# Attention with mixed heads: the scores and the product with v in four TensorE visits per row group

## The chip, the cores and the metric

The kernel runs on one core of one Trainium2 chip. The metric is the device time in microseconds (us) of one execution; the median of three executions stands for the kernel. Engines: TensorE (PE; PEld is its weight load), VectorE (DVE), ScalarE (ACT), GpSimd (POOL), SyncE (SP, which here only issues DMAs).

## The reference, cut to what matters

```python
scores = scale * q @ k.T                            # 4 batches, 12 heads, 448 x 448, head size 64
scores = einsum('bhij,hg->bgij', scores, w_pre)     # first mixing, over the heads
attn = softmax(scores)                              # max, exp, sum, divide
attn = einsum('bgij,gf->bfij', attn, w_post)        # second mixing, over the heads
x = attn @ v                                        # "a times v", then 1792 tokens x 768
x = ((x @ w1) * (x @ w2)) @ w3 @ w_out
out = square(relu(x @ w_in)) @ w_out2
```

Everything is float32 at the borders. Products are made in three terms of high and low halves.

## The kernel before, in words

**Row groups and blocks.** Each batch has four row groups of 110, 110, 110 and 118 query rows (`SUP`, 16 in all, called s). A row group is cut into blocks of ten rows (the last one may have eight; `BLK`, 180 in all, called u). A block holds 10 rows x 12 heads = 120 partitions, so that both mixings over the heads are matmuls with a 120 x 120 matrix. `first[s]` is the first block of row group s. A row group lasts 11 or 12 blocks.

**What happens to a row group.** `qk(s, p)` (line 228) makes the scores of a pair of heads p (six pairs) into one PSUM tile of two banks of which there is one (`ps_s`); its six matmuls work on the two halves of 64 rows of the array. `evict_s` (line 246) copies them on ScalarE into the row group's tile S. `regroup(u)` (line 274) brings ten rows of all heads by a DMA on SyncE's queue into the tile Bt (five buffers). Then per block: `premix` (line 281, the first mixing, TensorE, into one of three PSUM tiles p), `negmax` (VectorE), `expo` (ScalarE), `norm` (VectorE), `split_h` (GpSimd; on ScalarE for some blocks while k is split) and `split_l` (VectorE for even blocks, GpSimd for odd ones) make the halves EH and EL, `postmix` (line 371, the second mixing, TensorE, into one of two PSUM tiles o), `at_h` (ScalarE) and `at_l` (VectorE) raise the result into the halves ATh and ATl. When all blocks of a row group are there, `av(s, p, part)` (line 477) multiplies by v: 24 matmuls for a pair of heads, each on 64 columns of the array, three pairs of heads into the one PSUM tile a. `put_xh` (ScalarE) and `put_xl` (VectorE) take x out of it as two halves, `store_x` (SyncE) writes them to memory.

**The order.** It is written by hand. A loop over slots u (line 1320) issues in each slot: loads; `at_h` of block u - 5; in odd slots the first mixing of blocks u + 1 and u + 2; `negmax(u)`; events of the kind FIRST; `expo(u)`; the norms and splits of blocks u - 2 and u - 3; the second mixing of block u - 4; `at_l` of block u - 5; events of the kinds MID and LOW; events of the kind END; last `regroup(u + 5)`. Every engine works through its instructions in this order. The events (from line 546) say in which slot the pieces of `qk`, `evict_s`, `av` and so on stand. Before, the six pieces of `qk` of row group s are spread evenly over a row group's slots (`qs`, line 557), one to a slot, the copy `evict_s` one slot later; the pieces of `av` of an earlier row group stand in the same slots behind them (`at_qk`, line 597). A visit below is a slot in which TensorE leaves the mixings for `qk` or `av`.

**Other pieces that the change touches.** `load_q`, `split_q` and `split_ql` run nine, five and four slots ahead of the score pieces that need them. The k of the next batch is loaded and split in slots `ks` (line 571). `scale_v` (line 439) finds the scale of v by two small matmuls, for which it borrows the bank of the a tile. `split_v` and `split_vl` split v for row group 4b.

Of the kernel before, what the change touches and what calls it, by code (L numbers as in the profile page):

```python
# [18 lines left out]
P = 128  # L19
CP = 112  # L20
F64_BIAS = 2.0 ** -112
NR = 10
ROWS = (110, 110, 110, 118)
LEAD = 5
LAG = 4
EG = 7
EW = 66
TB = 4
# [6 lines left out]
def talking_heads_attention_moe_moe2(  # L35
# [55 lines left out]
    def psum(pool, tag, dt=F32):  # L91
        return pool.tile([P, 512], dt, tag=tag, name=tag)
# [346 lines left out]
    def scale_v(b, i):  # L439

        m = vsum[b]
        if i == 0:
            nc.vector.tensor_reduce(m[:CP, 6:7], m[:CP, 0:6], axis=AX.X, op=ALU.max)
        elif i == 1:
            t = pav[4 * b - 1, 1] if b else psum(ps_a, "a")
            vps[b] = pt = t[:, 512 - P :]
            nc.tensor.transpose(pt[:1, :CP], m[:CP, 6:7], ident[:CP, :CP])
        elif i == 2:
            nc.vector.tensor_reduce(m[:1, 7:8], vps[b][:1, :CP], axis=AX.X, op=ALU.max)
        elif i == 3:  # L450
            nc.tensor.matmul(vps[b][:, :1], ones[:1], m[:1, 7:8], start=True, stop=True)
        else:
            up, lo = pow2(vps.pop(b)[:, :1], 14, "vs")
            nc.vector.tensor_scalar(
                xs[:, b : b + 1], lo, wunscale, 2.0 ** XSH, op0=ALU.mult, op1=ALU.mult
            )
            Vsc[b] = up
# [87 lines left out]

    events = {}
    LOAD, FIRST, MID, LOW, END = range(5)

    def at(slot, kind, f, *a):
        events.setdefault(slot, []).append((kind, len(events), f, a))  # L550

    low_k, crowded, copies = set(), set(), []
    for s in range(2, NSUP):
        b = SUP[s][0]
        base = first[s - 1]
        L = first[s] - base
        qs = [base - 4 + p * L // NDC for p in range(NDC)]
        made = list(qs)
        if s == 2:
            made[:3] = base - 5, base - 2, base - 1  # L560
        for p in range(NDC):
            at(made[p], END, qk, s, p)
            copies.append((base - 2 if s == 2 and p == 0 else made[p] + 1, s, p))
            if p % 3 == 0:
                at(qs[p] - 9, LOAD, load_q, s, p // 3)
                at(qs[p] - 5, MID, split_q, s, p // 3, None)
                if p == 0 and qs[p] - 4 in low_k:
                    crowded.add(qs[p] - 3)
                at(qs[p] - 4 + (qs[p] - 3 in crowded), LOW, split_ql, s, p // 3)
        if s % 4 == 0:  # L570
            ks = [(first[s - 2] + 4) // 2 * 2 + 2 * p for p in range(NDC)]
            full.update(range(ks[0], ks[-1] + 4))
            for p in range(NDC):
                assert ks[p] + 1 < qs[p]
                at(ks[p], MID, split_k, b, p, None)
                at(ks[p] + 1, LOW, split_kl, b, p)
                low_k.add(ks[p] + 1)
                at(ks[p] - 4, LOAD, load_k, b, p)
    for slot, s, p in copies:
        at(slot, MID if slot in crowded else FIRST, evict_s, s, p)  # L580
    for b in range(B):
# [3 lines left out]
        for hg in range(2):  # L585
            for i in range(3):
# [3 lines left out]
                if b == B - 1:  # L590
                    at(f + 3 * hg + i + 13, MID, split_v, b, hg, i)
                    at(f + 3 * hg + i + 14, LOW, split_vl, b, hg, i)
    qk_at = sorted(x for x in events if any(e[2] is qk for e in events[x]))
    for s in range(NSUP - 1):
        for p in range(NDC):
            lo = first[s + 1] + LAG + 1
            at_qk = [x for x in qk_at if lo <= x < lo + SUP[s + 1][3]]
            slot = at_qk[p] if len(at_qk) == NDC else lo + (0, 1, 3, 5, 6, 7)[p]
            if s % 4 == 0 and s < NSUP - 4:
                b = SUP[s][0]  # L600
                assert slot - 2 > first[s] + 13
                at(slot - 2, MID, split_v, b, *divmod(p, 3))
                at(slot - 1, LOW, split_vl, b, *divmod(p, 3))
            for part in range(2):
                at(slot, END, av, s, p, part)
            if p % 3 == 2:
                at(slot + 1, FIRST, put_xh, s, p // 3)
                at(slot + 1, MID, put_xl, s, p // 3)
                if s < NSUP - 2:
                    at(slot + 2, END, store_x, s, p // 3)  # L610

    for b in range(B):
        for i, slot in ((1, 10), (3, 12)):
            at(first[4 * b] + slot, END, scale_v, b, i)

    last = NSUP - 1
    for p in range(NDC):
        for part in range(2):
            at(first[last] + TB + LAG + 1 + (2 * p + part) * (NB - first[last] - TB) // 12,
               END, av, last, p, part, (0, TB * NR))  # L620


    order = ExitStack()
# [693 lines left out]

    mlp_start = first[NSUP - 1] - 4
    early = iter(())
    for u in range(NB + LAG + 2):  # L1320
        if u == NB - LEAD:
            limit[0] = len(chunks)
            load_to(2 + LOADS)
        if u == mlp_start:
            kst.close()
            pools["w"] = ctx.enter_context(tc.tile_pool(name="wp", bufs=2, side="right"))
        if u in W_LOADS:
            load_to(W_LOADS.index(u) + 1)
        if u == c0:
            early = (x for x in pair_steps(0, None) if x[2])  # L1330
        if u - mlp_start in X_HIGH:
            load_x(0, X_HIGH.index(u - mlp_start))
        if u == NB - LEAD + 1:
            for b in range(B):
                load_x(1, b)
        work = sorted(events.pop(u, []), key=lambda e: e[0])

        def do(now):
            for kind, _, f, a in work:
                if kind == now:  # L1340
                    f(*a)

        do(LOAD)
        if 0 <= u - LAG - 1 < NB - LAG:
            at_h(u - LAG - 1)
        if u in AHEAD:
            postmix(u - LAG)
        if u % 2:
            for x in (u + 1, u + 2):
                if x < NB:  # L1350
                    premix(x)
        if u in FILL:
            keep_busy(FILL[u])
        if u < NB:
            negmax(u)
        do(FIRST)
        if u < NB:
            expo(u)
        if u % 2 == 0 and 0 <= u - 2 < NB:
            norm(u - 2)  # L1360
        if 0 <= u - 2 < NB:
            split_h(u - 2)
            if low_on_pool(u - 2):
                split_l(u - 2)
        if 0 <= u - 3 < NB and not low_on_pool(u - 3):
            split_l(u - 3)
        if 0 <= u - LAG < NB and u not in AHEAD:
            postmix(u - LAG)
        if 0 <= u - LAG - 1 < NB - LAG:
            at_l(u - LAG - 1)  # L1370
        do(MID)
        do(LOW)
        for eng, cost, f in islice(early, STEPS.get(u, 0)):
            f()
        do(END)
        if NB <= u < NB + LAG:
            assert next(early, None) is None
            allow[0] = place["w1", 2]
            at_h(u - LAG)
            at_l(u - LAG)  # L1380
            first_tile(u - NB)
        if u + LEAD < NB:
            regroup(u + LEAD)
# [923 lines left out]
```

## Time and profile before

| | |
|---|---|
| median of three runs | 1222.35 us (1222.11 to 1223.85) |
| profiled execution | 1222.48 us, span 1220.8 us |
| TensorE busy | 1206.9 us, 99% of the span |
| VectorE, ScalarE, GpSimd busy | 948.8, 804.5, 587.6 us |
| TensorE's clock | granted in full in all 40 slices of the span |
| attention | about the first 430 us; the MLPs behind it |

The span reaches from the first to the last instruction, the time of an execution a little further. A line such as L380 is a line of the kernel: L284 is the first mixing, L380 the second, L241 the scores, L494 a times v, L248 the score copy, L396 and L402 the raising into ATh and ATl. In a timeline a record is an instruction, or several alike (x2); the records of one engine overlap, because matmuls are pipelined, so starts are compared with starts. In the chain of waits each piece is the time by which the work that ended last was carried by that line.

### The profile page before, as it was taken

The numbers are of one execution on the slowest core, as the hardware profiler recorded it, in microseconds if no ns is written. First come the engines' busy times: TensorE is split into PE (matmuls) and PEld (weight loads), VectorE is DVE, ScalarE is ACT, GpSimd is POOL, SyncE is SP. The second block draws the span as 40 slices with busy tenths as digits, with TensorE's granted clock in tenths as the row PEclk, the third lists the DMA queues.
The fourth block names the chain that finished last, engine by engine and source line by source line (L and its number), as shares of the span: only waits on it lengthen the run. The fifth ranks groups of instructions, "written<-read, shape, count | busy, mean of one in ns | idle before, by whom it ended". The sixth has DMA issues, their size and how long they took to land.

```text
span 1220.8 us, 26222 instructions
## 1 busy us (share of the span) xinstructions
PE 1206.9 (99%) x9904; PEld 746.7 (61%) x9904; DVE 948.8 (78%) x1690; ACT 804.5 (66%) x1620; POOL 587.6 (48%) x569
## 2 busy tenths in 40 slices
PE   8999999999999999999999999999999999999998
PEld 3666676676676665555557985555555555666665
DVE  6988899888889956766675876697778775999773
ACT  6887888878888735654464545567878876654430
POOL 3898788889879510110001311446233424666340
PEclk9999999999999999999999999999999999999999
DMA  6466555655645843755543537344478659656562
GB/s 193 129 161 163 138 146 132 171 126 155 172 119 162 242 128 95 175 127 156 134 134 112 189 120 242 127 159 166 160 251 290 240 185 314 207 162 187 171 196 79
DMA packets 139843, 205.02 MB, mean 168 GB/s; under 512 B 33764, under 2 KB 114788, under 8 KB 139716
## 3 DMA queue, kind: packets, MB, share of 16 engines
q1 hardware_dynamic: 136020, 200.01, 55.4%
q10 hardware_dynamic: 3136, 2.40, 0.8%
q8 instruction: 78, 1.28, 0.4%
q0 software_dynamic: 560, 0.93, 0.4%
q14 instruction: 49, 0.40, 0.1%
HBM read 114.60 MB, written 50.16 MB: 135 GB/s over the span
## 4 chain that ended last, share of the span: by engine, by line
PE 90%; DMA 4%; DVE 3%; ACT 1%; issue 0%; SPq 0%; ACTq 0%; POOL 0%
PE mm L1248 25%; PE mm L2113 16%; PE mm L1861 16%; PE p L284 9%; PE o L380 7%; PE mm L1525 5%; PE s L241 5%; PE a L494 4%; DMA Bt<-S 2%; PE p L1248 2%; DVE ATl L402 1%; DMA x<-x_d 1%; DVE EL L367 1%; DVE st L298 1%; ACT E L306 0%; DMA vraw<-in_v_dram 0%
## 5 line engine op out<-in xcount | busy, mean ns | idle before, releaser
L1248 PE MATMUL mm<-x,w 128*128 128x448 f16 x1044 | 197.7, 352 | 0.0
L1248 PEld LDWEIGHTS <-w 128*128 128x128 f16 x1152 | 112.2, 98 | 105.2 <-issue 1.0
L1861 PE MATMUL mm<-x,wq 128*128 128x448 f16 x882 | 169.2, 352 | 0.0
L284 PE MATMUL p<-Bt,wpre_k 120*120 120x448 f32 x360 | 159.4, 560 | 5.7 <-DMA Bt<-S 3.1
L2113 PEld LDWEIGHTS <-ao 128*128 128x128 f16 x1176 | 115.0, 98 | 76.0
L380 PEld LDWEIGHTS <-EH 120*112 120x112 f16 (+1 forms) x1440 | 124.3, 130 | 44.6 <-issue 37.2
L353 POOL TENSOR_SCALAR EH<-E,st 120x448 f16<-120x448 f32 (+1 forms) x152 | 113.0, 751 | 47.7 <-DVE st L336 35.6
L1861 PEld LDWEIGHTS <-wq 128*128 128x128 f16 x882 | 86.0, 98 | 79.6
L402 DVE TENSOR_TENSOR ATl<-o,ATh 112x480 f16<-112x480 f32 x180 | 116.1, 645 | 23.9 <-ACT ATh L396 22.9
L396 ACT CAST ATh<-o 112x480 f16<-112x480 f32 x180 | 101.2, 562 | 45.7 <-PE o L380 40.7
L306 ACT ACTIVATE E<-p,st 120x448 f32<-120x448 f32 x180 | 116.1, 645 | 21.5 <-DVE st L298 13.1
L380 PE MATMUL o<-wph,EH 120*112 120x120 f16 x720 | 124.1, 219 | 1.2 <-DVE ATl L402 1.1
L380 PE MATMUL o<-wph,EL 120*112 120x120 f16 x720 | 122.0, 216 | 0.0
L380 PE MATMUL o<-wpl,EH 120*112 120x120 f16 x720 | 122.0, 216 | 0.0
L365 POOL TENSOR_TENSOR EL<-F,EH 120x448 f16<-120x448 f32 (+1 forms) x90 | 104.6, 1162 | 33.7 <-issue 20.4
L298 DVE TENSOR_REDUCE st<-p 120x1 f32<-120x448 f32 x180 | 110.2, 612 | 2.6 <-PE p L284 2.4
L1248 PE MATMUL mm<-h,M 128*128 128x448 f16 x576 | 110.2, 353 | 0.0
L2113 PE MATMUL mm<-x,ao 128*128 128x384 f16 x588 | 96.5, 326 | 0.0
L2113 PE MATMUL mm<-ow,ao 128*128 128x384 f16 x588 | 96.0, 326 | 0.0
L380 PEld LDWEIGHTS <-EL 120*112 120x112 f16 x720 | 93.6, 130 | 0.0
L367 DVE SCALAR_TENSOR_TENSOR EL<-E,st,EH 120x448 f16<-120x448 f32 (+1 forms) x90 | 82.9, 921 | 10.3 <-POOL EH L353 9.9
L1248 PEld LDWEIGHTS <-M 128*128 128x128 f16 x576 | 55.9, 98 | 52.0 <-DVE M L1435 0.8
(264 smaller groups left out, 2535.1 us busy)
## 6 DMA issues: line engine op xcount, KB each, us to landing
Bt<-S SPq DMA_DIRECT2D x176, 210.0 KB
raw<-in_moe_w_out_dram SPq DMA_DIRECT2D x24, 768.0 KB
g<-ev SPq DMA_DIRECT2D x64, 224.0 KB
gt<-g SPq DMA_DIRECT2D x56, 256.0 KB
raw<-in_moe_w_in_dram SPq DMA_DIRECT2D x16, 768.0 KB
raw<-in_moe_w_dram SPq DMA_DIRECT2D x14, 768.0 KB
raw<-in_moe_w_dram SPq DMA_DIRECT2D x16, 512.0 KB
kept_out<-xa SPq DMA_DIRECT2D x16, 384.0 KB
```

Of the source, the lines that this page charges most:

```text
L284: nc.tensor.matmul(pt[: n * H, :S], wpre_k.rearrange("p t g -> p (t g)")[: n * H, : n * H], Bt.pop(u)[: n * H], start=True, stop=True,)
L298: nc.vector.tensor_reduce(nsum[u][:n, 0, j : j + 1], Pp[u][:n, :S], axis=AX.X, op=ALU.max, negate=True)
L306: nc.scalar.activation(e[:n], Pp.pop(u)[:n, :S].rearrange("p (a b) -> p a b", a=EG), AF.Exp, bias=t[:n, 0, j : j + 1], scale=1.0, accum_ou ...
L353: nc.gpsimd.tensor_scalar(seven(EH[u][:n]), Ex[u][:n], inverse(u), 1.0, op0=ALU.mult, op1=ALU.mult)
L365: nc.gpsimd.tensor_tensor(a, f, b, op=ALU.subtract)
L367: nc.vector.scalar_tensor_tensor(a, e, inverse(u), b, op0=ALU.mult, op1=ALU.subtract)
L380: nc.tensor.matmul(pt[:CP, c * n : (c + 1) * n], a[:n, c * CP : (c + 1) * CP], w[:n, :n], start=(i == 0), stop=(i == 2),)
L396: nc.scalar.copy(ATs[s][0][:, :, :, m * NR : m * NR + nr], src)
L402: nc.vector.tensor_tensor(ATs[s][1][:, :, :, a], src, ATs[s][0][:, :, :, a], op=ALU.subtract)
L1248: nc.tensor.matmul(pt[:, :S], w[a][:, cs], x[z][:, sl], start=(c == 0 and i == 0), stop=(c == len(parts) - 1 and i == 2),)
L1861: nc.tensor.matmul(pt[:, :S], w[:, a, c * P : (c + 1) * P], xop(t, b, kb, c), start=(start and c == 0 and m == 0), stop=(c == 2 and m == 2 ...
L2113: nc.tensor.matmul(pt[:, :OH], y[:, a, q * P : (q + 1) * P], ow[g, q][kb][:, w], start=(start and q == 0 and m == 0), stop=(q == NQ - 1 an ...
```

## The change

From row group 3 on, the six score pieces stand in four visits: a, a + 3, a + 6 and at most a + 9, where a is the first odd slot from `first[s - 1]` - 4 on. In slots a and a + 6 there is a double visit: a score piece, its copy `evict_s` at once in the same slot, all three pairs of heads of `av` for one half (hg) of row group s - 3, then a second score piece, whose copy follows in the next slot behind `expo`. In a + 3 and in the last one stands a single score piece. `early_high` calls `at_h` of block u - 4 in the slot of the double visit, ahead of the copy, and not at the start of the next slot. For row groups 13 and 14, which have no scores beside them, `av` stands in two visits and not in six. In a slot behind a slot with a visit, `postmix` comes ahead of `premix`. The splits of v come in neighbouring slots, `ks` starts two slots earlier, `scale_v` takes a PSUM tile of its own ring, and kinds END to END + 3 order scores, a times v, second scores, and stores with `scale_v`.

```diff
--- before.py
+++ after.py
@@ -442,8 +442,7 @@
         if i == 0:
             nc.vector.tensor_reduce(m[:CP, 6:7], m[:CP, 0:6], axis=AX.X, op=ALU.max)
         elif i == 1:
-            t = pav[4 * b - 1, 1] if b else psum(ps_a, "a")
-            vps[b] = pt = t[:, 512 - P :]
+            vps[b] = pt = psum(ps_a, "a")[:, 512 - P :]
             nc.tensor.transpose(pt[:1, :CP], m[:CP, 6:7], ident[:CP, :CP])
         elif i == 2:
             nc.vector.tensor_reduce(m[:1, 7:8], vps[b][:1, :CP], axis=AX.X, op=ALU.max)
@@ -545,22 +544,41 @@
 
     events = {}
     LOAD, FIRST, MID, LOW, END = range(5)
+    raised = set()
+
+    def early_high(u):
+        if BLK[u][1]:
+            at_h(u)
+            raised.add(u)
 
     def at(slot, kind, f, *a):
         events.setdefault(slot, []).append((kind, len(events), f, a))
 
     low_k, crowded, copies = set(), set(), []
+    double, from_pool = {}, {}
     for s in range(2, NSUP):
         b = SUP[s][0]
         base = first[s - 1]
         L = first[s] - base
-        qs = [base - 4 + p * L // NDC for p in range(NDC)]
-        made = list(qs)
         if s == 2:
-            made[:3] = base - 5, base - 2, base - 1
+            qs = [base - 4 + p * L // NDC for p in range(NDC)]
+            made = [base - 5, base - 2, base - 1] + qs[3:]
+        else:
+            a = (base - 4) | 1
+            qs = made = [a, a, a + 3, a + 6, a + 6, min(a + 9, base + L - 6)]
+            double[s] = (a, a + 6)
         for p in range(NDC):
-            at(made[p], END, qk, s, p)
-            copies.append((base - 2 if s == 2 and p == 0 else made[p] + 1, s, p))
+            if made.count(made[p]) == 1:
+                at(made[p], END, qk, s, p)
+                copies.append((base - 2 if s == 2 and p == 0 else made[p] + 1, s, p))
+            elif p % 3 == 0:
+                at(made[p], END, early_high, made[p] - LAG)
+                at(made[p], END, qk, s, p)
+                at(made[p], END, evict_s, s, p)
+            else:
+                at(made[p], END + 2, qk, s, p)
+                copies.append((made[p] + 1, s, p))
+                crowded.add(made[p] + 1)
             if p % 3 == 0:
                 at(qs[p] - 9, LOAD, load_q, s, p // 3)
                 at(qs[p] - 5, MID, split_q, s, p // 3, None)
@@ -568,7 +586,7 @@
                     crowded.add(qs[p] - 3)
                 at(qs[p] - 4 + (qs[p] - 3 in crowded), LOW, split_ql, s, p // 3)
         if s % 4 == 0:
-            ks = [(first[s - 2] + 4) // 2 * 2 + 2 * p for p in range(NDC)]
+            ks = [(first[s - 2] + 2) // 2 * 2 + 2 * p for p in range(NDC)]
             full.update(range(ks[0], ks[-1] + 4))
             for p in range(NDC):
                 assert ks[p] + 1 < qs[p]
@@ -590,34 +608,32 @@
                 if b == B - 1:
                     at(f + 3 * hg + i + 13, MID, split_v, b, hg, i)
                     at(f + 3 * hg + i + 14, LOW, split_vl, b, hg, i)
-    qk_at = sorted(x for x in events if any(e[2] is qk for e in events[x]))
     for s in range(NSUP - 1):
+        b, lo = SUP[s][0], first[s + 1] + LAG + 1
         for p in range(NDC):
-            lo = first[s + 1] + LAG + 1
-            at_qk = [x for x in qk_at if lo <= x < lo + SUP[s + 1][3]]
-            slot = at_qk[p] if len(at_qk) == NDC else lo + (0, 1, 3, 5, 6, 7)[p]
+            hg, i = divmod(p, 3)
+            slot = double[s + 3][hg] if s + 3 in double else lo + (3, 7)[hg]
             if s % 4 == 0 and s < NSUP - 4:
-                b = SUP[s][0]
-                assert slot - 2 > first[s] + 13
-                at(slot - 2, MID, split_v, b, *divmod(p, 3))
-                at(slot - 1, LOW, split_vl, b, *divmod(p, 3))
+                assert slot - 4 > first[s] + 13
+                at(slot - 4 + i, MID, split_v, b, hg, i)
+                at(slot - 3 + i, LOW, split_vl, b, hg, i)
             for part in range(2):
-                at(slot, END, av, s, p, part)
-            if p % 3 == 2:
-                at(slot + 1, FIRST, put_xh, s, p // 3)
-                at(slot + 1, MID, put_xl, s, p // 3)
+                at(slot, END + 1, av, s, p, part)
+            if i == 2:
+                at(slot + 1, FIRST, put_xh, s, hg)
+                at(slot + 1, MID, put_xl, s, hg)
                 if s < NSUP - 2:
-                    at(slot + 2, END, store_x, s, p // 3)
+                    at(slot + 2, END + 3, store_x, s, hg)
 
     for b in range(B):
         for i, slot in ((1, 10), (3, 12)):
-            at(first[4 * b] + slot, END, scale_v, b, i)
+            at(first[4 * b] + slot, END + 3, scale_v, b, i)
 
     last = NSUP - 1
     for p in range(NDC):
         for part in range(2):
             at(first[last] + TB + LAG + 1 + (2 * p + part) * (NB - first[last] - TB) // 12,
-               END, av, last, p, part, (0, TB * NR))
+               END + 1, av, last, p, part, (0, TB * NR))
 
 
     order = ExitStack()
@@ -1317,6 +1333,7 @@
 
     mlp_start = first[NSUP - 1] - 4
     early = iter(())
+    turned = {x for x in events if any(y[2] in (qk, av) for y in events[x])}
     for u in range(NB + LAG + 2):
         if u == NB - LEAD:
             limit[0] = len(chunks)
@@ -1341,9 +1358,9 @@
                     f(*a)
 
         do(LOAD)
-        if 0 <= u - LAG - 1 < NB - LAG:
+        if 0 <= u - LAG - 1 < NB - LAG and u - LAG - 1 not in raised:
             at_h(u - LAG - 1)
-        if u in AHEAD:
+        if u in AHEAD or u - 1 in turned and 0 <= u - LAG < NB:
             postmix(u - LAG)
         if u % 2:
             for x in (u + 1, u + 2):
@@ -1364,7 +1381,7 @@
                 split_l(u - 2)
         if 0 <= u - 3 < NB and not low_on_pool(u - 3):
             split_l(u - 3)
-        if 0 <= u - LAG < NB and u not in AHEAD:
+        if 0 <= u - LAG < NB and u not in AHEAD and u - 1 not in turned:
             postmix(u - LAG)
         if 0 <= u - LAG - 1 < NB - LAG:
             at_l(u - LAG - 1)
@@ -1372,7 +1389,8 @@
         do(LOW)
         for eng, cost, f in islice(early, STEPS.get(u, 0)):
             f()
-        do(END)
+        for kind in range(END, END + 4):
+            do(kind)
         if NB <= u < NB + LAG:
             assert next(early, None) is None
             allow[0] = place["w1", 2]
```

## Rows read from the trace of the kernel before

**Rows 1.** Chain of waits, 300 to 345 us: shares by line, one piece (start, us, what)
```profile
by line: PE p L284 37.0%; PE o L380 28.4%; PE s L241 17.7%; PE a L494 16.9%; issue 0.1%
...
301.25 1.59 PE p L284 x4
```

**Rows 2.** Stretches: us, busy PE, PEld, DVE, ACT, POOL (xcount), clock, DMA share, GB/s
```profile
160.00:210.00 50.00, 49.53 (x665) 35.17 (x663) 46.79 (x96) 41.44 (x91) 45.05 (x48) 1.00 0.58 150
210.00:260.00 50.00, 50.00 (x647) 35.10 (x645) 41.19 (x94) 40.35 (x94) 39.64 (x47) 1.00 0.58 151
```

**Rows 3.** TensorE's timeline around one visit: start, us, what
```profile
303.26 0.22 PE L380 MATMUL o<-wph,EL 120*112 120x120 f16 x1
303.40 0.45 PE L241 MATMUL s<-kh,qh 64*110 64x448 f32 x2
303.69 0.37 PE L241 MATMUL s<-kl,qh 64*110 64x448 f32 x2
303.90 0.37 PE L241 MATMUL s<-kh,ql 64*110 64x448 f32 x2
304.20 0.24 PE L494 MATMUL a<-ATh,Vh 112*64 112x110 f16 x2
304.27 0.22 PE L494 MATMUL a<-ATl,Vh 112*64 112x110 f16 x2
...
304.75 0.22 PE L494 MATMUL a<-ATh,Vl 112*64 112x110 f16 x2
304.90 0.26 PE L380 MATMUL o<-wph,EH 120*112 120x120 f16 x1
305.00 0.22 PE L380 MATMUL o<-wpl,EH 120*112 120x120 f16 x1
```

**Rows 4.** Chain of waits, 400 to 470 us: start, us, what
```profile
400.30 0.63 PE o L380 x12
400.93 0.70 PE a L494 x24
401.63 0.77 PE o L380 x12
...
404.07 7.56 DMA Bt<-S
...
421.40 8.20 DMA x<-x_d
```

**Rows 5.** TensorE's timeline, scores followed by the first mixing
```profile
47.81 0.37 PE L241 MATMUL s<-kh,ql 64*110 64x448 f32 x2
48.11 1.76 PE L284 MATMUL p<-Bt,wpre_k 120*120 120x448 f32 x4
```

**Rows 6.** Groups by line, 150 to 400 us: ScalarE's score copy (busy us, mean ns, idle before)
```profile
L248 ACT COPY S<-s 110x896 f32<-110x896 f32 (+1 forms) x56 | 51.2, 914 | 4.7 <-PE s L241 4.3 <-DMA vraw<-in_v_dram 0.2
```

**Rows 7.** VectorE's timeline: the low half of xt
```profile
218.56 0.50 DVE L522 SCALAR_TENSOR_TENSOR xt<-a,xt 128x330 f16<-128x330 f32 x1 [0.82 <-DMA Bt<-S]
```

**Rows 8.** SyncE's timeline: DMA issues
```profile
220.48 0.82 SPq L278 DMA_DIRECT2D Bt<-S  x1
...
295.61 1.47 SPq L203 DMA_DIRECT2D qraw<-in_q_dram  x1
297.18 0.82 SPq L278 DMA_DIRECT2D Bt<-S  x1
```

**Rows 9.** All of TensorE's waits, 60 to 400 us: total us, times, longest
```profile
PE o L380 <- DVE ATl L402: 0.8, 2, 0.5
PE p L284 <- ACT E L306: 0.2, 1, 0.2
PE p L284 <- ACT ATh L396: 0.2, 1, 0.2
```

**Rows 10.** GpSimd's timeline: two low halves of k
```profile
300.67 1.12 POOL L196 TENSOR_TENSOR kl<-kraw,kh 128x448 fp32r<-128x448 f32 x1
...
305.01 2.09 POOL L196 TENSOR_TENSOR kl<-kraw,kh 128x448 fp32r<-128x448 f32 x1
```

## The prediction

> **What bounds the kernel now.** I read the page's engine table first: TensorE is the busiest engine by far. Busy is not the same as bound, so next the chain of waits over 300 to 345 us, a stretch of the attention: its line of shares holds four TensorE lines and 0.1% of anything else [rows 1]. Third, the table by stretches says who would be next: between 160 and 260 us TensorE has half a microsecond of idle time in a hundred, VectorE is at 46.79 and 41.19 of 50 us, and GpSimd at 45.05 and 39.64 [rows 2]. So a microsecond taken from TensorE in the attention is a microsecond of time, as long as VectorE, GpSimd and the deliveries of the tile Bt can follow; the first two have 6% to 21% in hand.
>
> Fourth, TensorE's own timeline, start to start, shows what could be taken. Inside a kind of matmul the starts are regular [rows 3]: 0.05 us in the second mixing (0.63 for twelve [rows 4]), 0.21 in the scores (303.69 to 303.90), 0.048 in a times v (ten pairs of records from 304.27 to 304.75). At each border between kinds something is lost:
> - second mixing into scores: 0.14 instead of 0.05, and the first scores pair holds 0.29 instead of 0.21: 0.17;
> - scores into a times v: 0.30 instead of 0.21, and 0.07 instead of 0.05: 0.11;
> - a times v into second mixing: 0.15 instead of 0.05, and 0.10 instead of 0.05: 0.15. The chain gives 0.77 for such a mixing against 0.63 [rows 4], so I use 0.14;
> - second mixing into a times v alone: 0.70 for 12 pairs that need 0.58 [rows 3, 4]: 0.12;
> - scores into the first mixing: 0.30 instead of 0.21 [rows 5]; what the first mixing itself then loses doesn't show in that row. I take 0.14 in all, as on leaving a times v; at 0.09, the least, the sum below would be 2.7 us better (53 more such borders after than before).
>
> **The change, part by part.** *Borders.* Written out from the slot tables of both versions, the old order enters scores 84 times, goes on from there to a times v 79 times, enters a times v alone 16 times, leaves a times v 95 times and leaves scores for something else 5 times: 84 x 0.17 + 79 x 0.11 + 16 x 0.12 + 95 x 0.14 + 5 x 0.14 = 38.9 us. The new order has 26 double visits (13 row groups, two each: scores, three heads' a times v, scores), 32 visits with scores alone and 11 with a times v alone: 58 x 0.17 + 26 x 0.11 + 26 x new + 58 x 0.14 + 11 x 0.12 + 11 x 0.14 = 23.7 + 26 x new. The new border, a times v into scores, is in no row. Its nearest rows are 0.11 (scores into a times v) and 0.31 (leaving for the mixing and entering from it, 0.14 + 0.17); I take 0.17, the entry into scores, since what follows the border is the same instruction. That makes 28.1 us, **10.8 us saved**, between 7.1 and 12.3. (The Trainium skill, TensorEngine Tiling (Array Packing), section Key Properties, says that a change of tiling mode drains the engine, and a change of tile within a mode does not. By it the new border is one drain; it gives no duration, and with one drain priced as entry into scores the sum stays 10.8.)
>
> *Where that doesn't count.* From 404 us on, the chain runs through deliveries, Bt from 404.07 and x until 429.60 [rows 4]. Four of the six visits for row group 14 disappear inside that stretch, 4 x 0.26 = **1.0 us** that I take off.
>
> *The second scores piece of a double visit* needs the one score buffer, so ScalarE must copy the first piece out while TensorE does a times v. If it is late, TensorE stops, and behind it the next second mixing. The first piece ends about 0.9 us after the mixing before it, the copy takes 0.91 [rows 6], a times v runs for 1.75 us (36 pairs). ScalarE has 0.56 us of raising (at_h, now called ahead of the copy) to do in the first 0.9. It is left with 0.8 us: nothing is paid, unless ScalarE comes 0.8 us late. After the visit its work bunches: the xt copy can't start before a times v ends, then the exponential, the second copy and the next raise stand in line. VectorE's subtraction for ATl comes as much later, and the mixing two slots on needs that output buffer. Counted through with these durations it holds with a tenth or two to spare; I cost it at nothing beside the next item, which falls in the same place.
>
> *Bt and SyncE's queue.* The work between visits is now uneven. From the end of the mixing before a double visit: visit 0.89 + 1.75 + 0.17 + 0.63 + 0.14 = 3.58, mixing 0.63; a pair of slots with first mixings 1.59, two mixings and a single visit (0.17 + 0.63 + 0.14), 3.79; a pair without a visit, 1.59 + 1.26 = 2.85; the next two first mixings start at 10.85 and about 11.65. Their Bt tiles are issued behind the store of xt, which waits for VectorE's xt. That is ready at 2.64 + 0.22 (last a times v) + 0.5 (ScalarE, taken as VectorE's for the same columns) + 0.50 [rows 7] = 3.86, and the next Bt went out 1.42 us after it (219.06 to 220.48 [rows 8]): at 5.3. Its own issue takes 0.82, and in two of three cases a load of q follows, 1.47 [rows 8]: the second Bt goes out at 7.6, with 4.05 us to land. How long a landing takes is in no row; the tile issued at 297.18 [rows 8] was used by the second first mixing of the pair at 301.25 [rows 1], at about 302.05, without a wait, so 4.87 bounds it. Missing are thus between 0 and 0.8 us in each half row group. Nothing else shortens the far end, and none of TensorE's waits between 60 and 400 us is one for Bt [rows 9], so most landings beat that bound; I take 0.15. 26 x 0.15 = **3.9 us** off.
>
> *VectorE and GpSimd.* 10.8 us over 13 row groups is 0.83 for one of about 25 us. The stretch of each batch in which k and v are split (some 60 us, as 150 to 210) would be asked to run 2.0 us shorter with VectorE at 94% already [rows 2]; the three v splits now stand in neighbouring slots, and the k splits start two slots earlier. Between nothing and all of it is lost; I take a quarter, 0.5 us for each of three batches, **1.5 us**.
>
> *At nothing:* the second mixing put ahead of the first behind a visit is an order on TensorE alone; it delays the first mixing by 0.63, which the three p buffers cover while VectorE still has a maximum to take, and otherwise it would be part of the 0.15. The k loads two slots earlier on SyncE's queue wait for the same splits, which are two slots earlier too. The bank that scale_v now takes for itself waits for the xt of the slot before, one slot of over 2 us earlier.
>
> **Sum:** 10.8 - 1.0 - 3.9 - 1.5 = 4.4 us. The profiled execution took 1222.48 us (span 1220.8), 0.13 above the median of the three runs: 1218.1 against the first, **1218.0 us** as a median. A measurement of this kernel can tell about 0.2%, 2.4 us, from no change.
>
> **The rivals.** *It all comes through:* landings stay under 4 us and VectorE follows: 10.8 - 1.0 = 9.8, 1212.5 (1211.0 with the new border at 0.11). For it: no wait on Bt between 60 and 400 us today. Against it: the 4.05 us are less than the only bound. Chance 0.20.
>
> *No change, because VectorE and GpSimd become the bound:* all 2.0 us of the three split stretches are lost, 10.8 - 1.0 - 3.9 - 6.0 = -0.1, 1222.5. A GpSimd subtraction took 1.12 us once and 2.09 another time [rows 10], so work there grows when it is squeezed against VectorE's. (The Trainium skill, SBUF — State Buffer, section SBUF: two separate sides, says that a VectorE operation with two SBUF inputs and a GpSimd operation hold the shared ports exclusively, the other waiting for the whole instruction. By that rule their two busy times cannot be packed closer, which is this rival.) The same time comes out where *the change doesn't do what it says*: if the new border costs 0.31, the sum is 7.1 - 1.0 - 5.4 = 0.7, 1221.7. Together 0.20.
>
> *Slower:* each double visit holds SyncE's queue (the store waits for xt, the q load and Bt stand behind it), and the Bt for the next double visit lands late by 0.7 us, as the 4.87 allow. 26 x 0.7 = 18.2: 1222.4 - 9.8 + 18.2 = 1230.8. It decides from (10.8 - 1.0) / 26 = 0.38 us a half group on. For it: Bt landings of 7.56 us appear when the queues are full [rows 4]. Against it: up to 400 us the first mixing is not held now. Chance 0.20.
>
> **How the numbers follow.** The forecast (1215.2 to 1219.9) has 0.40. Faster by over 0.2% is 0.40 + 0.20 = 0.60, within it 0.20, slower 0.20. The likeliest case's own range is 1215 to 1220; the range for 8 in 10 runs from 1212.0, a little inside the best end, to 1226.0, which takes in the unchanged case and the near part of the slower one; outside stay some 0.05 below and 0.13 above.
>
> **What would show it.** Right: in TensorE's timeline two scores pieces round 72 records of a times v, the border between at 0.17 more than the regular step, and the row-group period shorter by 0.3 to 0.8 us. TensorE's waits show Bt for the first mixing behind a pair without a visit, a few us in total. Wrong: the border at 0.25 or more; waits of scores on the score copy (ScalarE late by over 0.8 us); second mixing held by ATl or EL for more than a microsecond a row group, which would put the bound on VectorE or GpSimd; or Bt waits of 10 us and more, which would make it slower. If the gain shows at 400 us but not at the end, the delivery stretch took it.

## The result: 1.4% slower

The changed kernel takes 1239.12 us (1237.43 to 1243.01), the kernel before, beside it, 1222.97: a ratio of 1.0137, 95% interval 1.0108 to 1.0165, 16 us more where 4.4 less was forecast. The profiled execution took 1240.67 us, its span is 1239.0. The lines of the page, then the chain of waits over the same 45 us as in [rows 1], then the stretches of [rows 2]:

```profile
span 1239.0 us, 26227 instructions
PE 1205.0 (97%) x9904; PEld 743.4 (60%) x9904; DVE 940.1 (76%) x1690; ACT 802.9 (65%) x1620; POOL 585.9 (47%) x569
```

```profile
by line: PE p L284 21.9%; PE o L380 19.2%; PE a L493 12.5%; DMA Bt<-S 11.0%; PE s L241 10.6%; ACT E L306 6.3%; DVE EL L367 4.7%; issue 4.2%; ACT S L248 3.4%; DVE ATl L402 2.6%; ACT ATh L396 2.2%; POOL EH L353 1.4%; ACT EH L351 0.7%
```

```profile
160.00:210.00 50.00, 43.80 (x538) 29.72 (x536) 38.48 (x84) 35.31 (x77) 38.86 (x40) 0.93 0.52 134
210.00:260.00 50.00, 48.41 (x656) 33.75 (x655) 38.38 (x85) 40.45 (x96) 38.77 (x47) 1.00 0.55 142
```

In the first stretch every engine has become less busy: VectorE fell from 46.79 to 38.48 us of 50, GpSimd from 45.05 to 38.86, TensorE from 49.53 to 43.80. In the second ScalarE alone stays where it was (40.45 us, 40.35 before). The chain, once TensorE alone, is TensorE's for only 64% of its time now; the rest passes through eight other kinds of pieces and "issue". TensorE's waits over the stretch of [rows 9], once 1.2 us, are now these:

```profile
PE o L380 <- DVE ATl L402: 9.3, 9, 2.0
PE p L284 <- DMA Bt<-S: 6.0, 5, 2.4
PE p L284 <- ACT E L306: 3.3, 7, 0.6
```

The borders themselves came out as priced. TensorE's timeline of a double visit (start, us, what):

```profile
264.41 0.37 PE L241 MATMUL s<-kh,ql 64*110 64x448 f32 x2
264.70 0.24 PE L493 MATMUL a<-ATh,Vh 112*64 112x118 f16 x2
...
266.54 0.23 PE L493 MATMUL a<-ATh,Vl 112*64 112x118 f16 x2
266.69 0.46 PE L241 MATMUL s<-kh,qh 64*110 64x448 f32 x2
266.99 0.37 PE L241 MATMUL s<-kl,qh 64*110 64x448 f32 x2
267.19 0.37 PE L241 MATMUL s<-kh,ql 64*110 64x448 f32 x2
267.49 0.26 PE L380 MATMUL o<-wph,EH 120*112 120x120 f16 x1
267.59 0.22 PE L380 MATMUL o<-wpl,EH 120*112 120x120 f16 x1
```

The new border loses 0.10 up to the scores (0.15 for 0.05) and 0.09 in their first pair (0.30 for 0.20 to 0.21), 0.19 here for the 0.17 taken. Scores into the mixing lose 0.09 and 0.05, the 0.14 taken. Counted in the trace, scores are entered 84 times before and 84 after, but 26 of these from a times v and 58 from the mixings, which is the slot table of the prediction. So by price and count the 10.8 us are there, less half a us if all 26 new borders cost 0.19.

What ate them I counted from all matmul starts up to the last second mixing: the time by which a step from start to start exceeds the regular step of its kind. Before it sums to 7.2 us, after to 33.8. The last second mixing comes 18.3 us later (442.49 to 460.77): 26.6 us more standing, less 10.8, is 15.8, and the other 2.5 us are not placed. TensorE ran part of this time at the lower clock (last section), and the count can't tell a matmul that is slow from one that waits. The standing is everywhere, 0.5 to 3 us for most ten slots, and thick in the stretch with the k split: about 6 us in slots 70 to 79, part of it slow matmuls.

One of the thick places reads as follows. GpSimd's timeline, VectorE's, TensorE's, all of the changed kernel:

```profile
310.20 1.45 POOL L226 TENSOR_TENSOR ql<-qraw,qh 128x330 fp32r<-128x330 f32 x1
311.62 1.12 POOL L196 TENSOR_TENSOR kl<-kraw,kh 128x448 fp32r<-128x448 f32 x1
312.73 0.63 POOL L353 TENSOR_SCALAR EH<-E,st 120x448 f16<-120x448 f32 x1
```

```profile
313.39 1.05 DVE L367 SCALAR_TENSOR_TENSOR EL<-E,st,EH 120x448 f16<-120x448 f32 x1 [1.95 <-POOL EH L353]
314.37 0.65 DVE L402 TENSOR_TENSOR ATl<-o,ATh 112x480 f16<-112x480 f32 x1
```

```profile
315.06 0.21 PE L380 MATMUL o<-wph,EH 120*112 120x120 f16 x1 [2.00 <-DVE ATl L402]
```

GpSimd makes two low halves before EH; VectorE waits 1.95 us for EH with ATl behind it in order; the second mixing waits 2.00 us for the output buffer that ATl frees. But GpSimd, too, comes late to its two low halves. Just before them it stood idle:

```profile
308.41 0.69 ACT L351 ACTIVATE EH<-E,st 120x448 f16<-120x448 f32 x1
```

```profile
309.24 1.01 POOL L365 TENSOR_TENSOR EL<-F,EH 120x448 f16<-120x448 f32 x1 [2.25 <-DMA Bt<-S]
```

The view names Bt for these 2.25 us, but the EL of an odd block reads EH, which ScalarE makes in this stretch and had ready at 309.10; ScalarE had the score copy (306.56), ATh and an exponential ahead of it. So the wait that TensorE feels has passed from ScalarE over GpSimd and VectorE.

The same handing on is behind most of TensorE's waits for ATl. Between 40 and 440 us they sum to 11.8 us in 13 waits (1.1 in 3 before), and seven of them, 9.0 us, end within 2.6 us behind the start of an EL on VectorE that itself had waited over 0.3 us for GpSimd's EH. VectorE's waits for EH in the same stretch:

```profile
DVE EL L367 <- POOL EH L353: 14.3, 14, 2.0
```

SyncE is caught by the same queue (its timeline, and the landing as TensorE saw it):

```profile
183.61 0.48 SPq L203 DMA_DIRECT2D qraw<-in_q_dram  x1
187.26 0.35 SPq L180 DMA_DIRECT2D kraw<-in_k_dram  x1
187.70 1.69 SPq L278 DMA_DIRECT2D Bt<-S  x2
```

```profile
193.47 1.82 PE L284 MATMUL p<-Bt,wpre_k 120*120 120x448 f32 x2 [1.74 <-DMA Bt<-S]
```

The k load goes out at 187.26, when GpSimd's kl of 186.09 to 187.23 has freed its buffer, and two Bt stand behind it. Between 60 and 400 us SyncE stood three times like this, 11.1 us in all.

### The profile page after: what moved, and what is told of

Same layout as the page of the kernel before. It is cut to its first block, busy times and chain, and to the rows that moved or that the text cites. A ratio compares the mean times of both kernels' runs of the same rounds, so it can differ in the third digit from the quotient of the medians.

```text
span 1239.0 us, 26227 instructions
## 1 busy us (share of the span) xinstructions
PE 1205.0 (97%) x9904; PEld 743.4 (60%) x9904; DVE 940.1 (76%) x1690; ACT 802.9 (65%) x1620; POOL 585.9 (47%) x569
## 4 chain that ended last, share of the span: by engine, by line
PE 83%; DMA 6%; DVE 5%; ACT 4%; issue 1%; POOL 0%; SPq 0%; POOLq 0%
PE mm L1264 25%; PE mm L2131 15%; PE mm L1879 15%; PE p L284 6%; PE mm L1543 5%; PE o L380 5%; DMA Bt<-S 5%; PE a L493 4%; PE s L241 3%; ACT E L306 2%; PE p L1264 2%; DVE ATl L402 1%; DVE EL L367 1%; DVE Vl L472 1%; ACT S L248 1%
## 5 line engine op out<-in xcount | busy, mean ns | idle before, releaser
L284 PE MATMUL p<-Bt,wpre_k 120*120 120x448 f32 x360 | 162.3, 563 | 14.0 <-DMA Bt<-S 9.2
L380 PE MATMUL o<-wph,EH 120*112 120x120 f16 x720 | 126.2, 220 | 13.1 <-DVE ATl L402 11.8
L365 POOL TENSOR_TENSOR EL<-F,EH 120x448 f16<-120x448 f32 (+1 forms) x90 | 100.7, 1118 | 44.8 <-issue 17.6
L284 PEld LDWEIGHTS p<-Bt,wpre_k 120*120 120x120 f32 x360 | 56.5, 183 | 59.3 <-issue 24.5
L367 DVE SCALAR_TENSOR_TENSOR EL<-E,st,EH 120x448 f16<-120x448 f32 (+1 forms) x90 | 78.3, 870 | 15.6 <-POOL EH L353 15.4
```

The source lines that it names most:

```text
L284: nc.tensor.matmul(pt[: n * H, :S], wpre_k.rearrange("p t g -> p (t g)")[: n * H, : n * H], Bt.pop(u)[: n * H], start=True, stop=True,)
L365: nc.gpsimd.tensor_tensor(a, f, b, op=ALU.subtract)
L367: nc.vector.scalar_tensor_tensor(a, e, inverse(u), b, op0=ALU.mult, op1=ALU.subtract)
L380: nc.tensor.matmul(pt[:CP, c * n : (c + 1) * n], a[:n, c * CP : (c + 1) * CP], w[:n, :n], start=(i == 0), stop=(i == 2),)
```

## The experiments

Theories, as the runs went on: **A**, GpSimd's and SyncE's queues in the k split; **B**, the unevenness of TensorE's visits as such: in the pairs of slots without a visit the other engines can't follow, and in the double visits they run dry; **C**, the k move alone; **D**, the order of the mixings; **E**, x, whose two halves wait in order for the end of three heads' a times v (22.1 us on ScalarE and 22.5 on VectorE between 60 and 400 us). The kernel before, run beside each of them, took 1222 to 1223 us.

### The low half of k left out, in both kernels

```diff
-        ll = kq.tile([P, S], F32R, tag="kl", name="kl", bufs=8)
+        ll = hh if b else kq.tile([P, S], F32R, tag="kl", name="kl", bufs=8)
...
         hh, ll = kT[b, p]
+        if b:
+            return
         nc.gpsimd.tensor_tensor(ll, kraw[b, p // 2][:, p % 2, :], hh, op=ALU.subtract)
```

> The changed kernel without the low halves of k for batches 1 to 3: GpSimd makes no kl there and the matmuls that read kl read kh instead, so TensorE's work stays the same. Theory A (GpSimd's queue: kl and ql stand ahead of EH, VectorE waits for EH with ATl behind it, the second mixing waits for ATl; SyncE's k load waits for kl with Bt behind it): the losses of the k stretches, some 12 us, go, and the time comes to 1223 to 1229 us. Theory B (the uneven visits outrun VectorE, ScalarE and Bt everywhere, k or not): no more than 4 us go, 1235 us or more.

> The kernel before with the same left out (no kl for batches 1 to 3), as a control. Both theories: TensorE is the bound there and keeps its work, so within 2 us of 1222.4. If it falls by as much as the changed kernel does, that run says nothing about the change.

The changed kernel came to 1233.01 us, ratio 1.0073 (1.0054 to 1.0093); the control to 1220.55, 0.9977 (0.9968 to 0.9986). So the k split holds some 6 us of the loss, 3.6 more than it is worth to the kernel before: theory A is half of what it promised, and 12 us remain between the two without it. The time fell into neither expected range. Part of the 6 us can be the clock: without kl the four executions ran at a granted clock of 0.998 to 1.0, the changed kernel's at 0.996 to 0.997.

### The k split early, and the order of the mixings

```diff
-            ks = [(first[s - 2] + 4) // 2 * 2 + 2 * p for p in range(NDC)]
+            ks = [(first[s - 2] + 2) // 2 * 2 + 2 * p for p in range(NDC)]
```

> The kernel before with the k splits and loads two slots earlier and nothing else of the change. If the move of the k splits alone (theory C) piles kl onto ql and the v splits, 1226 us or more with waits of the second mixing on ATl; theories A and B need the uneven visits as well: 1221 to 1225 us.

1228.36 us, ratio 1.0042 (1.0027 to 1.0057): moved by two slots, in an otherwise unchanged kernel, the k split, with its loads, costs 5 us by itself, theory C. TensorE's waits in this kernel, 40 to 440 us:

```profile
PE p L284 <- DMA Bt<-S: 3.2, 6, 1.1
PE o L380 <- DVE ATl L402: 2.7, 3, 1.2
PE p L284 <- ACT E L306: 1.9, 3, 0.9
```

In the changed kernel the other order was tried:

```diff
-    turned = {x for x in events if any(y[2] in (qk, av) for y in events[x])}
+    turned = set()
```

> The changed kernel with the first mixing ahead of the second in every slot again, as before the change. Theory D (putting the second mixing first makes the first mixing, and with it VectorE's maximum and the exponential, late by 0.63 us): 1234 us or less. Theories A and B: the order is no cause; within 4 us of 1239, and rather above, since the second mixing then comes later behind a visit.

1242.83 us, ratio 1.0163 (1.0134 to 1.0192). Theory D falls; the second mixing first does no harm, and whether it helps the two intervals don't tell.

### x later, q away from k

```diff
-                at(slot + 1, FIRST, put_xh, s, hg)
-                at(slot + 1, MID, put_xl, s, hg)
+                at(slot + 1, LOW, put_xh, s, hg)
+                at(slot + 2, LOW, put_xl, s, hg)
                 if s < NSUP - 2:
-                    at(slot + 2, END + 3, store_x, s, hg)
+                    at(slot + 3, END + 3, store_x, s, hg)
```

> The changed kernel with x taken later: ScalarE's high half of xt behind the second score copy in the slot after the double visit, VectorE's low half and the store each one slot later. Theory E (xt: both halves stand in order ahead of the next blocks' work and wait for the end of three heads' a times v, 25.6 us of waits on ScalarE and 25.8 on VectorE in the changed kernel; VectorE, idle then, becomes the bound in the pairs of slots without a visit): those waits fall below 10 us and the time by 5 us or more, to 1234 or less. If only GpSimd's k queue counts (theory A): within 3 us of 1239.

> The same, and the low halves of k left out for batches 1 to 3 as before (kh read in their place). Theories A and E together, each by itself: 1233 less what xt gives, 1228 or less, and 1217 if nothing else holds TensorE. Theory B (unevenness as such: too few buffers between the visits, whatever stands where): 1230 or more.

1242.58 us (1.0149 to 1.0206) and, without the low half of k, 1233.12 (1.0076 to 1.0106) where the changed kernel without it had 1233.01. Theory E falls as far as it blames x alone. ScalarE, rid of the wait for x, waits for the second score piece instead, and ATl as much later (waits of the first of the two, 40 to 440 us):

```profile
DVE ATl L402 <- ACT ATh L396: 45.4, 29, 3.1
ACT S L248 <- PE s L241: 30.9, 39, 1.3
```

In these two versions what stands first in the order waits for the visit to end, x or the score copy. Next, the low halves of q moved off those of k for row groups 4, 8, 12:

```diff
-                at(qs[p] - 9, LOAD, load_q, s, p // 3)
-                at(qs[p] - 5, MID, split_q, s, p // 3, None)
-                if p == 0 and qs[p] - 4 in low_k:
-                    crowded.add(qs[p] - 3)
-                at(qs[p] - 4 + (qs[p] - 3 in crowded), LOW, split_ql, s, p // 3)
+                apart = s % 4 == 0
+                back = 3 if apart and p == 0 else 0
+                at(qs[p] - 9 - back, LOAD, load_q, s, p // 3)
+                at(qs[p] - 5 - back, MID, split_q, s, p // 3, None)
+                at(qs[p] - (3 if apart and p else 4) - back, LOW, split_ql, s, p // 3)
```

> The changed kernel with the low halves of q moved out of the k split for row groups 4, 8 and 12: the first half three slots earlier with its load, ahead of the first low half of k, the second one slot later, in a slot without one. Theory A in its narrow form (ql right beside kl is what puts EH off on GpSimd): the 2 us waits of the second mixing on ATl in the k stretches go, 4 to 6 us less, 1233 to 1235. If kl alone is enough for it, or theory E holds everything: 1237 or more.

> Both edits. If the causes are separate the gains add: 1228 or less. If both act through the same late VectorE, the sum of the two single gains isn't reached.

1238.33 us (1.0114 to 1.0144) and 1237.44 (1.01 to 1.014): not told apart from the changed kernel. So ql right beside kl is not what costs the expected 4 us or more. Nor is GpSimd full there: in the first of the two it is busy for 41.59 us between 160 and 210 us, less than in the kernel before (45.05).

### VectorE relieved, and both relieved

```diff
+        if not low_on_pool(u):
+            EL[u] = EH[u]
+            return
         EL[u] = bp.tile([NBK, S], F16, tag="EL", name="EL", bufs=4)
```

> The changed kernel with VectorE's low half EL of the even blocks left out (the second mixing reads EH in its place, so TensorE's work is the same): VectorE has 0.93 us less in each pair of slots, 2.8 instead of 3.75, under TensorE's 2.85 of a pair without a visit. Theory B (between the double visits TensorE asks for two blocks in 2.85 us, and VectorE's 3.75 can't follow, idle as it was during the visit): the waits on ATl and on the exponential fall by half or more and the time to 1228 or less. If GpSimd or the deliveries hold TensorE: 1233 or more.

> Control: the same left out of the kernel before. TensorE is the bound there: 1219 to 1223 us by all theories.

> The changed kernel without EL of even blocks and without the low halves of k. Theories A and B together hold the whole loss: 1212 to 1217 us, the time that the saved borders alone would give. If 1222 or more, a third cause holds TensorE in the visits or pairs (ScalarE's order, Bt).

Without EL of the even blocks the changed kernel takes 1231.58 us (1.0046 to 1.0089), the control 1222.79 (0.9986 to 1.0008). So this EL is worth nothing to the kernel before and 7.5 us to the changed one. The first expectation's 1228 was missed, though in the profiled execution (1228.43 us, the fastest of four) the standing of a second mixing behind a first (by the count from start to start) fell from 11.9 us to 2.4. The run doesn't say why EL costs: leaving it out takes 0.93 us of work a pair off VectorE, and it also ends VectorE's wait for GpSimd's EH, the 14.3 us above.

With both left out, 1226.21 (1222.06 to 1229.23 in ten executions; 1.0011 to 1.0041): 13 us of the 16, and still not below the kernel before. The two gains, 6.1 and 7.5 us by themselves, nearly add. The ten executions spread with the clock: the five with a granted clock of 0.999 or 1.0 took 1222.06 to 1226.07 us, the five at 0.995 to 0.997 took 1226.35 to 1229.23. What holds TensorE then is what the prediction had made its main loss (waits of this kernel, 25 to 440 us, in an execution of 1222.14, one of the fastest):

```profile
PE p L286 <- DMA Bt<-S: 7.9, 10, 2.0
PE p L286 <- DVE ATl L407: 1.8, 4, 0.5
PE p L286 <- ACT E L308: 1.3, 3, 0.6
```

### Unevenness alone

One part of the change, put into the kernel before: three heads' a times v in one visit (scale_v with a PSUM tile of its own, as in the change), everything else where it was.

```diff
-            for part in range(2):
-                at(slot, END, av, s, p, part)
             if p % 3 == 2:
+                for j in range(p - 2, p + 1):
+                    for part in range(2):
+                        at(slot, END, av, s, j, part)
```

> The kernel before with one part of the change alone: a times v of three heads' pairs in one visit, twice a row group, in the slots of the third and the sixth score piece; the six score pieces, their copies and the k split stay where they are. Borders for a row group: 2 x 0.42 + 4 x 0.31 = 2.08 us instead of 2.57, 6 us in all, and every pair of slots keeps a visit (3.79 us or more for TensorE). Theory B: nearly all of it comes, 1216 to 1219. If three heads at once are the cause by themselves (x late, a times v holding the mixings): 1224 or more.

1233.71 us, ratio 1.0086 (1.0071 to 1.0101), where 1216 to 1219 were expected. Without a double visit, without a move of the k split, and though its pairs of slots keep a visit, it loses 11 us. TensorE's waits there, 40 to 440 us, mainly carry the three names from above and a fourth, the score copy:

```profile
PE o L380 <- DVE ATl L402: 6.4, 10, 1.2
PE p L284 <- ACT E L306: 3.1, 8, 0.6
PE p L284 <- DMA Bt<-S: 2.3, 4, 0.8
PE s L241 <- ACT S L248: 1.8, 6, 0.7
```

x (theory E) or unevenness of a lesser degree could be the cause, so x was put late in this kernel too, where no second score piece can take its place:

```diff
-                at(slot + 1, FIRST, put_xh, s, p // 3)
-                at(slot + 1, MID, put_xl, s, p // 3)
+                at(slot + 1, LOW, put_xh, s, p // 3)
+                at(slot + 2, LOW, put_xl, s, p // 3)
                 if s < NSUP - 2:
-                    at(slot + 2, END, store_x, s, p // 3)
+                    at(slot + 3, END, store_x, s, p // 3)
```

> The kernel with three heads' a times v in one visit (1233.7 us) with x taken later: ScalarE's half behind the exponential of the next slot, VectorE's half and the store one slot later. The score copy isn't held in this one. Theory E (x stands waiting ahead of the blocks' work): 5 us or more less, 1228 or less. Theory B: within 3 us of 1233.7.

1237.67 us (1.0107 to 1.0135): 4 us worse than with x early. And the plain test of theory B, the kernel before with the same six visits, bunched:

```diff
         made = list(qs)
+        if s > 2 and s % 4:
+            qs = [base - 4 + o for o in (0, 1, 2, 5, 6, 9)]
+        made = list(qs)
```

> The kernel before with its six visits a row group kept as they are (one score piece and one head pair's a times v each, the same borders, x one slot behind), but bunched in ten of the thirteen row groups: slots 0, 1, 2, 5, 6, 9 from the first instead of 0, 1, 3, 5, 7, 9, so that two pairs of slots in a row group have no visit and others two. Theory B (unevenness as such): 6 us or more slower, 1228 or more, with waits on ATl, the exponential and Bt behind the pairs without a visit. If three heads at once or the late x are what costs, 1221 to 1225.

1228.62 us, ratio 1.0045 (1.0032 to 1.0059). In its trace TensorE changes its kind of matmul as often as before (84 entries into scores, 79 of them on to a times v). Six microseconds are lost because two of the six visits stand one slot earlier (slots 2 and 6 for 3 and 7), with what the code hangs on them: the score copy, x of one half with its store, and pieces of the v split. Its waits, 60 to 400 us, have the same three names as those of the changed kernel:

```profile
PE o L380 <- DVE ATl L402: 3.1, 5, 1.4
PE p L284 <- DMA Bt<-S: 1.0, 1, 1.0
PE p L284 <- ACT E L306: 0.4, 1, 0.4
```

Last, a mild form that could have beaten both kernels:

```diff
-            for part in range(2):
-                at(slot, END, av, s, p, part)
+            for j in ((p,), (), (p - 1, p))[p % 3]:
+                for part in range(2):
+                    at(slot, END, av, s, j, part)
```

> The kernel before with the second head pair's a times v of each three moved one visit on: visits of scores with one, none, two head pairs. Four borders into and out of a times v fewer for a row group: 0.27 us each of 13, 3.5 us. It is mildly uneven (3.79, 4.45 and 5.06 us of TensorE for a pair of slots). Theory B: half of the 3.5 us or more is lost again, 1220 to 1224; if only three heads at once cost, 1218.5 to 1220.

1226.64 us, ratio 1.0033 (1.0021 to 1.0045): it lost not half of its 3.5 us but all of it and 4.5 us more. Here, too, scores wait for the score copy, 1.6 us in five waits between 60 and 400 us, which the kernel before never does there. No version that does all of the work is faster than the kernel before.

## Why the prediction was wrong

- **What bounds the kernel: right, but read too far.** TensorE was the bound, and the borders were saved nearly as counted: 0.19 at the new border for the 0.17 taken, 0.14 on leaving scores, 84 entries. But the chain left TensorE once the borders were gone, so a microsecond taken from it was no longer one of time.
- **"VectorE and GpSimd ... 1.5 us": the step that failed.** It judged from shares over 50 us, 6% to 21% in hand, that the other engines would follow, and took a loss in the k stretches alone. What the runs showed instead: engines with time in hand still hold TensorE, because each works in order and hands its lateness on. TensorE waited 11.8 us for ATl, 9.0 of it behind an EL that waited for EH, and VectorE and GpSimd were less busy than before. Two visits moved by one slot are enough for 6 us. EL left out gave 7.5 us back here and none before.
- **Why uneven visits do this** is argued, not shown. VectorE needs 3.75 us of a pair of slots (two maxima, two ATl, one EL, the norms); before, TensorE needed 4.45 in nearly every pair, and the change makes it 6.4, 3.8 and 2.85 in turn. What VectorE can't do in the long pair, because TensorE's mixings have not produced it, it would have to make up in the short one, with only two o and three p buffers between. The rows for this stood in the sums of the Bt step; they were used for Bt alone. But the sum by pairs is not the whole: the two kernels with three or two heads' pairs of a times v in a visit keep 3.79 us or more in every pair, and still lost 11 and 4.5 us.
- **The k split "between nothing and all of it", inside the same 1.5 us, and "at nothing" for its loads.** Two slots alone cost 5 us in the kernel before; with the low half of k left out 6 us came back. The bound was set wrong too: I let the loss be at most what was saved there (2.0 us a batch), as if a stretch couldn't become slower than it had been.
- **Bt: right in kind, short in size.** 3.9 us were taken, 6.0 us of waits measured between 60 and 400 us. One of the five waits, 1.74 us, has another cause: not the store behind x, but a k load that waits for GpSimd. The longest, 2.35 us before 397.63, has no k load ahead of it in SyncE's queue.
- **The second score piece: right by itself.** TensorE waited for a score copy once, 0.2 us between 40 and 440 us. What was priced at nothing beside it, ScalarE's bunching and the later ATl, is part of the waits above, and cost.
- **The signs it named for being wrong** didn't show one by one: the new border stayed under 0.25, scores hardly waited for the copy, Bt waits stayed under 10 us, and 11.8 us of ATl waits over 13 row groups are 0.9 a row group, just under the microsecond given. The loss came from all of these together.
- **The rivals.** The slower one had the side (1230.8 at 0.20) but named SyncE's queue, a third of the waits. The one with VectorE and GpSimd as the bound came nearest to the mechanism, though it asked for full engines, and was held at 1222.5. For it the prediction cited the Trainium skill, SBUF — State Buffer, section SBUF: two separate sides, on the ports that VectorE and GpSimd share. The trace agrees in part: VectorE's EL took 0.68 us at 307.03, where GpSimd stood idle, and 1.05 at 313.39, beside GpSimd's F. But the rule as cited is for operations with two SBUF inputs, so of VectorE's work in a pair it touches EL, and not the maxima or ATl, which take an input from PSUM. No run here tells how much of the 16 us is that rule and how much is mere queueing.
- **What stays open.** The reliefs and the bunched kernel show that the loss is the other engines' and comes with uneven visits and the moved k split. How the 16 us divide isn't known: A and B nearly add (6.1 and 7.5 us, 12.9 with both), but B's relief mixes VectorE's work with its wait for GpSimd; C's 5 us were measured in the kernel before and may be part of A's; and no run has the change with the k split left in its place. Why three heads' a times v in one visit costs 11 us, and why x taken late makes that kernel 4 us worse, stays open. In the kernel with both reliefs the last 4 us over the kernel before are put down to Bt and the clock by its waits and its executions' clocks alone.

## What to carry to other kernels

Where one engine is the bound at 99% and three others run at 79% to 94% beside it, the even alternation of its work can be what lets the others keep up. Before work of the bounding engine is bunched to save switches, set its time for each short stretch, here a pair of slots, against what every other engine needs in that stretch, and follow the order on each engine to see what a late piece holds up behind it; a share over 50 us didn't show it. The sum by pairs alone isn't enough: two kernels here passed it and lost. And the price of such a move isn't bounded by what it saves: a loss of 16 us came from a saving of 11.

## What was not expected of the hardware

TensorE's clock fell behind single stops of about 2 us, in a stretch that is otherwise busy. TensorE stood for 1.84 us up to 189.56, worked on, and ran at the lower of the two levels, 1.2 instead of 2.4 GHz, from about 190.5 to 197 us; the second stop, 1.74 us up to 193.47, falls within that. It was so again from about 398.5 to 402 us, behind a stop of 2.35 us that ended at 397.63. Stops of 2.00 to 2.02 us that ended at 95.49, 209.04 and 315.06 had no such fall behind them. The stretches (the clock is the third number from the end):

```profile
186.00:190.00 4.00, 2.16 (x17) 1.17 (x15) 2.12 (x4) 2.00 (x5) 3.92 (x6) 1.00 0.33 97
190.50:197.00 6.50, 4.76 (x20) 2.42 (x20) 3.57 (x8) 2.58 (x7) 5.10 (x7) 0.50 0.62 158
197.50:200.00 2.50, 2.50 (x80) 2.24 (x78) 0.83 (x3) 1.34 (x3) 0.00 (x0) 1.00 0.11 27
398.50:402.00 3.50, 3.50 (x41) 2.77 (x41) 1.45 (x5) 1.46 (x2) 2.72 (x5) 0.52 0.24 80
```

In the first of the two the second mixing's starts lie 0.10 us apart (195.09 to 196.19) instead of 0.05. The scores behind it, where the clock comes back:

```profile
196.42 0.71 PE L241 MATMUL s<-kh,qh 64*110 64x448 f32 x2
196.93 0.52 PE L241 MATMUL s<-kl,qh 64*110 64x448 f32 x2
197.29 0.36 PE L241 MATMUL s<-kh,ql 64*110 64x448 f32 x2
```

The first scores pair holds 0.51 us to the next start where 0.29 to 0.30 is its measure, the second 0.36 for 0.21, the third is back. The kernel before ran all its span at the full clock; over the span of the changed one the mean is 0.996. The 4.76 and 3.50 us that TensorE was busy in the two stretches would have been about half at the full clock: an estimate of 4 us that the clock cost this execution, from these rows. So waits can cost twice, once as standing and once more as slow matmuls behind them.
